# Attention with a parallel MLP: the output tile in two halves, its maxima in pairs, and score-value bursts of four

## The chip, the cores and the metric

The kernel runs on one core of one Trainium2 chip. The metric is the device time of one execution in microseconds, median over runs. The profile is one further execution, taken by the hardware profiler; it has its own time.

A core has TensorE (PE, matrix products into PSUM; PEld is its loading of weights), ScalarE (ACT, exponentials and other functions), VectorE (DVE, element-wise work and 32 x 32 transposes), GpSimd (POOL) and SyncE (SP, here the issuer of nearly all DMAs). Each takes its instructions in the order of the program. PSUM holds what TensorE writes: here eight banks of 128 x 512 fp32 values.

## What is computed

x has 2048 rows of 448. The result is x + A(xn) + B(xn), with xn the layer norm of x.

```
xn = layernorm(x)
A: q = xn @ wq  (16 heads of 28),  k = xn @ wk, v = xn @ wv  (one head of 28, shared by all)
   p = softmax(q @ k.T * 28 ** -0.5);  A = concat(p @ v) @ wo
B: y = layernorm(xn);  B = gelu(y @ w1 + b1) @ w2 + b2       (448 -> 1792 -> 448)
out = x + A + B          (y is a norm of a norm: B normalises xn once more)
```

## The kernel before

The program has three stretches. The first normalises x, and makes queries, keys and values. The second is the MLP; its result, with x and b2 added, goes to memory as `ad`. The third, from about 344 us on, is the attention, and all of the change lies there.

**Units and steps.** A unit is a chunk of 512 query rows and a group of four heads: `NU` = 4 x 4 = 16 units, u = 0 to 15, chunk c = u // 4. A unit has 16 key tiles of 128 (`kt`), and for each key tile and each of the four heads (`j`) one score tile of 128 keys x 512 queries. The main loop (L904) goes over the units and, in each, over eight steps i = 0 to 7. The text calls them the first to the eighth.

**A score** (`score`, L695) is one matmul of 128 x 512 (L703) into a PSUM bank from `mtile`, and an exponential by ScalarE (L704) out of the bank into half of a pair tile `p`, of which there are `PAIRS` = 12. **A score-value product** (`pv`, L889) takes the four heads of one key tile: on TensorE it shows as 8 matmuls with 128 x 32 weights (L894), adding to the one bank `po` for the unit. They come in bursts at the end of a step (letter P): a burst of two key tiles is 16 matmuls. The value products run two key tiles behind the scores, so the burst of the first step ends the unit before.

**Maxima.** The exponent needs an upper estimate of each query's largest score. `max_job` (L529) multiplies the queries with the first 128 keys (matmul L533), transposes the bank to SBUF in 32 x 32 blocks (L540, into a tile `tt`) and takes maxima of the blocks (L541). It is run for unit u + 2 in unit u, one head per step, in the fourth to seventh step. `load_max` in the eighth step joins the maxima and sends their negatives into two rows of the query tile. The same `tt` tiles serve a unit later as scores of key tile 0: `shift_jobs(u + 1)` subtracts the maxima (VectorE, L545), takes the exponential (ScalarE, L548), and transposes back (VectorE, L554). It starts in the third step and goes on by one stage at each X or Y.

**PSUM banks.** `po` has one of the eight. `mtile` hands out the other seven in turn, three from the pool `mp` and four from `ring`, so that a request gets the bank of seven requests before. Scores, maxima and output tiles all come from there. A matmul into a bank waits until ScalarE (a score) or VectorE (a maximum, an output tile) has read what lay there.

**The output tile.** `o_part` (L774) multiplies the finished attention rows of the chunk before with wo: for 128 rows and four groups three matmuls each of 128 x 448 (L781 to L783, high and low parts), twelve in one bank. VectorE adds them to the row of `ad` in a tile `a` (L786), and SyncE sends it out (L787). Each unit from u = 4 on has one such tile, in the sixth step, in place of that step's burst; the seventh step then has a burst of four. The last chunk's four tiles come at the end (`end_jobs`).

**The normalisation** (`norm_jobs`, L818) of a finished unit goes step by step at the letter n: copy of `po` (L821), sum check (L800), transpose, reciprocal, transpose (L826 to L829), product (L832), rounding (L834) and, on GpSimd, the low part (L836).

**The order** inside a step is a string with one letter per action, written by hand; each engine then takes its share in that order. s is a score, M a maximum job, n one stage of the normalisation, X and Y one stage of the shift, e the joining of maxima, o the first output part of the last unit, and P the output tile or the burst:

```
ORDER = "YnsMssnsXsossseP"
SHARES = (8, 8, 8, 7, 7, 7, 7, 8)
```

`SHARES` are the scores of each step, 60 in a unit. SyncE fetches at the start of unit u the row of `ad` that the output tile needs (`load_rows_of`) and then the queries of unit u + 2 in four transfers (`load_q`).

Of the kernel before, what the change touches and what calls it, by code (L numbers as in the profile page):

```python
# [8 lines left out]
F32 = mybir.dt.float32  # L9
F32R = mybir.dt.float32r  # L10
AF = mybir.ActivationFunctionType
ALU = mybir.AluOpType
AX = mybir.AxisListType
PSUM = bass.MemoryType.PSUM

P = 128
S, D, H, DH, F = 2048, 448, 16, 28, 1792
NT = S // P
CT = 4
NCH = NT // CT  # L20
CW = CT * P
NG = H // 4
# [8 lines left out]
MLP_ORDER = (2, 3, 0, 1)  # L31
ENGINES = [mybir.EngineType.PE, mybir.EngineType.Activation, mybir.EngineType.DVE, mybir.EngineType.SP]
ORDER = "YnsMssnsXsossseP"
SHARES = (8, 8, 8, 7, 7, 7, 7, 8)
GELU = 0.044715, 0.7978845608028654
NH = 8
HD = D // 2
# [3 lines left out]
def block_kernel(ctx, tc, x, wq, wk, wv, wo, w1, b1, w2, b2, out):  # L41
    nc = tc.nc
    pe, act, dve, pool = nc.tensor, nc.scalar, nc.vector, nc.gpsimd
# [66 lines left out]
    def mtile(shape):  # L110
        if rings:
            given.append(0)
            if len(given) % 7 > 3 or len(given) % 7 == 0:
                return rings[0].tile(shape, F32, name="m")
        return mp.tile(shape, F32, name="m")
# [300 lines left out]
    for c, at in ((2, ((0, 1), (0, 2), (0, 2), (0, 3))), (3, ((1, 0), (1, 1), (1, 2), (1, 3)))):  # L416
        for k in range(CT):
            later(*at[k], lambda t=CT * c + k: bn(t))
        g = bn_end(c)
# [106 lines left out]
    def blocks_of(t):  # L526
        return t.rearrange("p (b i) -> p b i", i=32)

    def max_job(u, j):  # L529
        if j == 0:  # L530
            mrs[u] = keep.tile([P, 4 * NT], F32, name="mr2", bufs=2)
        pm = mtile([P, CW])
        pe.matmul(pm, km, qss[u][:, j, :], start=True, stop=True)  # L533
        if u == 0:
            if j == 0:
                lasts.append(f(xl_p.tile([P, 4, CW], F32R, name="xl")))
            tts[u, j] = lasts[0][:, j]
        else:
            tts[u, j] = att.tile([P, CW], F32, name="tt", bufs=5)
        dve.transpose(tts[u, j], pm)  # L540
        dve.tensor_reduce(mrs[u][:, NT * j:NT * j + NT], blocks_of(tts[u, j]), axis=AX.X, op=ALU.max)  # L541

    def first_shift(u, j):
        tt = blocks_of(tts[u, j])
# [219 lines left out]
    rows = {}  # L764

    def load_rows_of(c, tiles):
        for k in tiles:
            rows[c, k] = keep.tile([P, D], F32, name="a", bufs=4)
            dve.memset(rows[c, k][0:1, 0:1], 0.0)
            nc.sync.dma_start(rows[c, k], ad[:, CT * c + k, :])  # L770
# [3 lines left out]
    def o_part(c, k, gs):  # L774
# [9 lines left out]
        if gs[-1] == NG - 1:  # L784
            a = rows[c, k]
            dve.tensor_add(a, a, parts.pop((c, k)))  # L786
            (nc.scalar if k % 2 and c == NCH - 1 else nc.sync).dma_start(ov[:, CT * c + k, :], a)  # L787

    def o_jobs(c):
        for k in range(CT):  # L790
            o_part(c, k, range(NG))
            yield
# [107 lines left out]
    xside = Stream()  # L900
    pvq = [(u, kt) for u in range(NU) for kt in range(NT)]
    last = NU * NT // 2 - 1
    o_steps = {(u, 5): (u // NG - 1, u % NG) for u in range(NG, NU)}
    for u in range(NU):  # L904
        todo = [(u, kt, j) for kt in range(1 if u else 2, NT) for j in range(4)]
        for i in range(NT // 2):
            n = NT // 2 * u + i
            if n >= last - 1:
                load_rows_of(NCH - 1, (range(CT - 1), [CT - 1])[n - last + 1])
            for v, step in o_steps:  # L910
                if v == u and i == 0:
                    load_rows_of(o_steps[v, step][0], [o_steps[v, step][1]])
            if n == 9:
                load_wo()
            if 12 <= n < 12 + NG:
                prep_wo(n - 12)
            if i == 0 and u + 2 < NU:
                load_q(u + 2)
            jobs = todo[:SHARES[i] if u else 8 * (i > 0)]
            todo = todo[len(jobs):]  # L920
            maxima = [(u + 2, i - 3 - (u == 0))] if 3 + (u == 0) <= i < 7 + (u == 0) else []
            if u == 0 and i in (1, 2):
                maxima = [(1, 2 * i - 2), (1, 2 * i - 1)]
            for what in ORDER:
                if what == "s" and jobs:
                    score(*jobs.pop(0))
                elif what == "M":
                    for v, j in maxima:
                        if v < NU:
                            max_job(v, j)  # L930
                elif what in "XY":
                    if what == "X" and i == (2 if u else 3) and u + 1 < NU:
                        xside.add(shift_jobs(u + 1))
                    xside.step()
                elif what == "e":
                    if i == 7 and u + 2 < NU:
                        load_max(u + 2)
                    if n == 2:
                        load_max(1)
                elif what == "n":  # L940
                    side.step()
                elif what == "o":
                    if n == last:
                        o_part(NCH - 1, 0, range(NG - 1))
                elif what == "P":
                    assert not jobs
                    if (u, i) in o_steps:
                        o_part(*o_steps[u, i], range(NG))
                        continue
                    for _ in range((BURST if n else 0) * (1 + ((u, i - 1) in o_steps))):  # L950
                        pv(*pvq.pop(0))
        assert not todo
# [85 lines left out]
```

## Time and profile before

| | |
|---|---|
| median of 3 runs | 889.86 us (889.65 to 890.04) |
| profiled execution | 889.81 us, of which the span of the instructions is 888.0 us |
| granted TensorE clock, mean | 0.998 |
| busy share of the span: TensorE, ScalarE, VectorE, GpSimd | 99%, 79%, 55%, 8% |
| the costliest group: exponentials (L704), 956 of them | 489.8 us of ScalarE |
| score matmuls (L703), 960 | 268.8 us of TensorE |
| score-value matmuls (L894), 2016 | 239.9 us of TensorE |

Times inside the profile are microseconds from the start of the span. In a row of the timeline stand start, length, engine, line, operation, the tile written and the tiles read, the shape, how many instructions the row joins, and in brackets how long the engine rested before and what released it. A row of busy time in a window has the window, its length, and then busy time and number of instructions of TensorE, its weight loads, VectorE, ScalarE and GpSimd, followed by the granted clock, the share of DMA time and GB/s. The end of a matmul is modelled, and successive matmuls overlap; so the distance between starts is what counts on TensorE.

### The profile page before, as it was taken

The page shows a single profiled execution, that of the slowest core. Times are in us where ns is not written, and L with a number is a line of the kernel's source. Part 1 is how long each engine was busy: PE and PEld are TensorE (multiplying, and loading weights), DVE is VectorE, ACT ScalarE, POOL GpSimd, SP SyncE. Part 2 cuts the span into 40 slices and gives each one's busy share as a digit, 9 for nine tenths or more (in the row PEclk, how much of TensorE's full clock was granted, in tenths as well). Part 3 has the DMA queues.
Part 4 walks back from the last instruction along what each step waited for, and adds up shares of the span by engine and source line. Part 5 has one row for each costly group of instructions (what it writes and reads, how often), then busy time and mean ns, then how long its engine had stood idle before and what let it go on. Part 6 is the DMA issues. An engine that isn't in the chain of part 4 may idle for free.

```text
span 888.0 us, 13246 instructions
## 1 busy us (share of the span) xinstructions
PE 879.1 (99%) x4914; PEld 566.8 (64%) x4914; DVE 486.0 (55%) x963; ACT 701.7 (79%) x1334; POOL 73.1 (8%) x82
## 2 busy tenths in 40 slices
PE   9999999999999999999999999999999999999997
PEld 8778888888888887444444554554554554554555
DVE  6757766656556876555464464464463463463212
ACT  5677565545454466999999999999999999999992
POOL 5450000000000002040000000000000000000000
PEclk9999999999999999999999999999999999999999
DMA  9975232022003004031102202201202202200011
GB/s 294 326 250 182 94 117 83 1 94 96 1 5 111 1 11 125 2 79 43 43 1 54 64 11 53 64 11 54 63 11 54 64 11 53 63 12 12 21 36 61
DMA packets 36298, 60.69 MB, mean 68 GB/s; under 512 B 7783, under 2 KB 23349, under 8 KB 35205
## 3 DMA queue, kind: packets, MB, share of 16 engines
q1 hardware_dynamic: 34644, 58.95, 21.8%
q10 hardware_dynamic: 1584, 0.84, 0.4%
q8 instruction: 40, 0.66, 0.3%
q14 instruction: 30, 0.24, 0.1%
HBM read 39.89 MB, written 18.88 MB: 66 GB/s over the span
## 4 chain that ended last, share of the span: by engine, by line
PE 91%; ACT 6%; DVE 2%; issue 1%; DMA 0%; POOL 0%; SPq 0%; ACTq 0%; POOLq 0%
PE m L703 25%; PE po L894 24%; PE ph L178 12%; PE m L637 5%; PE m L640 5%; PE m L643 5%; ACT p L704 5%; PE qp L178 2%; PE m L533 2%; PE m L781 2%; PE m L783 1%; PE m L782 1%; PE ph L181 1%; PE ph L183 1%; PE m L406 1%; PE m L178 1%
## 5 line engine op out<-in xcount | busy, mean ns | idle before, releaser
L704 ACT ACTIVATE p<-m 128x512 f32<-128x512 f32 x956 | 489.8, 746 | 28.7 <-PE m L703 28.2
L703 PE MATMUL m<-xh,ks 128*128 128x512 f32 x960 | 268.8, 409 | 0.6 <-DVE tt L540 0.3
L703 PEld LDWEIGHTS m<-xh,ks 128*128 128x128 f32 x960 | 174.5, 188 | 139.7 <-ACT p L704 70.7
L894 PE MATMUL po<-p,vs 128*32 128x512 f32 x2016 | 239.9, 598 | 0.0
L894 PEld LDWEIGHTS po<-p,vs 128*32 128x32 f32 x2016 | 53.8, 109 | 119.7 <-issue 119.4
L610 ACT ACTIVATE hz<-hx,b1s 128x512 f32<-128x512 f32 x56 | 40.6, 726 | 103.0 <-DVE hx L607 103.0
L540 DVE STREAM_TRANSPOSE tt<-m 128x512 f32<-128x512 f32 x60 | 42.9, 715 | 94.9 <-PE m L533 94.9
L637 PE MATMUL m<-w2h,hh 128*128 128x448 f32 x224 | 81.9, 366 | 0.0
L640 PE MATMUL m<-w2l,hh 128*128 128x448 f32 x224 | 81.8, 365 | 0.0
L643 PE MATMUL m<-w2h,hl 128*128 128x448 f32 x224 | 81.7, 365 | 0.0
L821 DVE COPY oc<-po 128x512 f32<-128x512 f32 x15 | 10.4, 692 | 119.8 <-PE po L894 119.8
L607 DVE TENSOR_TENSOR hx<-ph,xn 128x512 f32<-128x512 f32 x53 | 36.5, 689 | 64.8 <-PE ph L183 64.7
L178 PE MATMUL ph<-xh,w1h 128*128 128x512 f32 x159 | 62.8, 395 | 0.0
L178 PE MATMUL ph<-xl,w1h 128*128 128x512 f32 x159 | 62.3, 392 | 0.0
L178 PE MATMUL ph<-xh,w1l 128*128 128x512 f32 x159 | 62.3, 392 | 0.0
L836 POOL TENSOR_TENSOR otl<-oc,oth 128x512 fp32r<-128x512 f32 x15 | 24.1, 1610 | 463.5 <-DVE oth L834 272.3
L548 ACT ACTIVATE tt<-tt 128x512 f32<-128x512 f32 x60 | 53.3, 888 | 0.0
L614 DVE SCALAR_TENSOR_TENSOR hz<-hz,hx 128x512 f32<-128x512 f32 x56 | 38.8, 693 | 20.9 <-ACT hx L611 20.9
L554 DVE STREAM_TRANSPOSE p<-tt 128x512 f32<-128x512 f32 x60 | 42.1, 702 | 9.4 <-ACT tt L548 9.3
L637 PEld LDWEIGHTS m<-w2h,hh 128*128 128x128 f32 x224 | 42.1, 188 | 5.0
L640 PEld LDWEIGHTS m<-w2l,hh 128*128 128x128 f32 x224 | 42.1, 188 | 4.6
L643 PEld LDWEIGHTS m<-w2h,hl 128*128 128x128 f32 x224 | 42.1, 188 | 3.5
(175 smaller groups left out, 1035.3 us busy)
## 6 DMA issues: line engine op xcount, KB each, us to landing
xh<-qd SPq DMA_DIRECT2D x64, 224.0 KB
qd<-qe SPq DMA_DIRECT2D x22, 256.0 KB
a<-in_A_x_dram SPq DMA_DIRECT2D x20, 224.0 KB
ad<-a SPq DMA_DIRECT2D x16, 224.0 KB
a<-ad SPq DMA_DIRECT2D x16, 224.0 KB
raw<-in_B_w_dram SPq DMA_DIRECT2D x7, 448.0 KB
out_dram<-a SPq DMA_DIRECT2D x14, 224.0 KB
xd<-xh SPq DMA_DIRECT2D x2, 1024.0 KB
```

The lines of the kernel that those rows point to most:

```text
L178: pe.matmul(ps, w, v, start=(n == 0), stop=False)
L540: dve.transpose(tts[u, j], pm)
L548: act.activation(tts[u, j], tts[u, j], AF.Exp, scale=SCALE)
L554: dve.transpose(p0s[u][:, j], tts.pop((u, j)))
L610: act.activation(hz, hx, AF.Square, bias=b1s[:, ft:ft + 1], scale=GELU[0] ** 0.5)
L614: dve.scalar_tensor_tensor(hz, hz, 1.0, hx, op0=ALU.add, op1=ALU.mult)
L637: pe.matmul(m2[k], hh[:, ts], w2h, start=(ft == 0), stop=False)
L640: pe.matmul(m2[k], hh[:, ts], w2l, start=False, stop=False)
L643: pe.matmul(m2[k], hl[:, ts], w2h, start=False, stop=(ft == NF - 1))
L703: pe.matmul(s, ks[:, kt * P:(kt + 1) * P], qss[u][:, j, :], start=True, stop=True)
L704: act.activation(p, s, AF.Exp, scale=SCALE)
L894: pe.matmul(po[32 * j:32 * j + 32, :], vs[:, kt, :], ps.pop((u, kt, j)), start=(kt == 0), stop=(kt == NT - 1))
```

## The change

From unit 4 on:

- The output tile is made in two halves of two head groups each (`o_half`): in the third step and in the fifth, each in a bank of its own, with an add of its own by VectorE. The row is sent after the second. The steps behind them, the fourth and the sixth, have bursts of four; so the unit has six bursts where it had seven.
- The four maxima of unit u + 2 are made in two pairs, in the third and fifth step; these steps have six scores each, all others eight.
- The steps follow new order strings. In the third and fifth step the reduction of the maxima (`tensor_reduce`) is put at the very end, after P and X (letter R), behind the transposes out of the banks and the half's add. In the other steps the shift stage that ScalarE works on stands behind four scores, not ahead of the first.
- The shift of unit u + 1 begins in the second step, not the third.
- `tt` has six buffers, not five.

```diff
--- before.py
+++ after.py
@@ -31,7 +31,9 @@
 MLP_ORDER = (2, 3, 0, 1)
 ENGINES = [mybir.EngineType.PE, mybir.EngineType.Activation, mybir.EngineType.DVE, mybir.EngineType.SP]
 ORDER = "YnsMssnsXsossseP"
+LATE_ORDERS = "nsssnsYsosssXeP", "nsMsnsYsmssPXR"
 SHARES = (8, 8, 8, 7, 7, 7, 7, 8)
+LATE_SHARES = (8, 8, 6, 8, 6, 8, 8, 8)
 GELU = 0.044715, 0.7978845608028654
 NH = 8
 HD = D // 2
@@ -526,7 +528,7 @@
     def blocks_of(t):
         return t.rearrange("p (b i) -> p b i", i=32)
 
-    def max_job(u, j):
+    def max_job(u, j, later=None):
         if j == 0:
             mrs[u] = keep.tile([P, 4 * NT], F32, name="mr2", bufs=2)
         pm = mtile([P, CW])
@@ -536,9 +538,16 @@
                 lasts.append(f(xl_p.tile([P, 4, CW], F32R, name="xl")))
             tts[u, j] = lasts[0][:, j]
         else:
-            tts[u, j] = att.tile([P, CW], F32, name="tt", bufs=5)
+            tts[u, j] = att.tile([P, CW], F32, name="tt", bufs=6)
         dve.transpose(tts[u, j], pm)
-        dve.tensor_reduce(mrs[u][:, NT * j:NT * j + NT], blocks_of(tts[u, j]), axis=AX.X, op=ALU.max)
+
+        def maxima(tt=tts[u, j]):
+            dve.tensor_reduce(mrs[u][:, NT * j:NT * j + NT], blocks_of(tt), axis=AX.X, op=ALU.max)
+
+        if later is None:
+            maxima()
+        else:
+            later.append(maxima)
 
     def first_shift(u, j):
         tt = blocks_of(tts[u, j])
@@ -786,6 +795,19 @@
             dve.tensor_add(a, a, parts.pop((c, k)))
             (nc.scalar if k % 2 and c == NCH - 1 else nc.sync).dma_start(ov[:, CT * c + k, :], a)
 
+    def o_half(c, k, gs):
+        po = mtile([P, D])
+        ts = slice(k * P, (k + 1) * P)
+        for g in gs:
+            oth, otl = ots[c, g]
+            pe.matmul(po, oth[:, ts], woh[:, g, :], start=(g == gs[0]), stop=False)
+            pe.matmul(po, oth[:, ts], wol[:, g, :], start=False, stop=False)
+            pe.matmul(po, otl[:, ts], woh[:, g, :], start=False, stop=(g == gs[-1]))
+        a = rows[c, k]
+        dve.tensor_add(a, a, po)
+        if gs[-1] == NG - 1:
+            nc.sync.dma_start(ov[:, CT * c + k, :], a)
+
     def o_jobs(c):
         for k in range(CT):
             o_part(c, k, range(NG))
@@ -900,36 +922,44 @@
     xside = Stream()
     pvq = [(u, kt) for u in range(NU) for kt in range(NT)]
     last = NU * NT // 2 - 1
-    o_steps = {(u, 5): (u // NG - 1, u % NG) for u in range(NG, NU)}
+    o_steps = {(u, 2 * h + 2): (u // NG - 1, u % NG, range(2 * h, 2 * h + 2)) for u in range(NG, NU) for h in range(2)}
     for u in range(NU):
         todo = [(u, kt, j) for kt in range(1 if u else 2, NT) for j in range(4)]
         for i in range(NT // 2):
             n = NT // 2 * u + i
             if n >= last - 1:
                 load_rows_of(NCH - 1, (range(CT - 1), [CT - 1])[n - last + 1])
-            for v, step in o_steps:
-                if v == u and i == 0:
-                    load_rows_of(o_steps[v, step][0], [o_steps[v, step][1]])
+            if i == 0 and u >= NG:
+                load_rows_of(u // NG - 1, [u % NG])
             if n == 9:
                 load_wo()
             if 12 <= n < 12 + NG:
                 prep_wo(n - 12)
             if i == 0 and u + 2 < NU:
                 load_q(u + 2)
-            jobs = todo[:SHARES[i] if u else 8 * (i > 0)]
+            jobs = todo[:(LATE_SHARES if u >= NG else SHARES)[i] if u else 8 * (i > 0)]
             todo = todo[len(jobs):]
             maxima = [(u + 2, i - 3 - (u == 0))] if 3 + (u == 0) <= i < 7 + (u == 0) else []
+            if u >= NG:
+                maxima = [(u + 2, i - 2), (u + 2, i - 1)] if i in (2, 4) else []
             if u == 0 and i in (1, 2):
                 maxima = [(1, 2 * i - 2), (1, 2 * i - 1)]
-            for what in ORDER:
+            reduces = []
+            for what in LATE_ORDERS[i in (2, 4)] if u >= NG else ORDER:
                 if what == "s" and jobs:
                     score(*jobs.pop(0))
-                elif what == "M":
+                elif what == "M" and u < NG:
                     for v, j in maxima:
                         if v < NU:
                             max_job(v, j)
+                elif what in "Mm":
+                    if u + 2 < NU:
+                        max_job(*maxima[what == "m"], reduces)
+                elif what == "R":
+                    for job in reduces:
+                        job()
                 elif what in "XY":
-                    if what == "X" and i == (2 if u else 3) and u + 1 < NU:
+                    if what == "X" and i == (1 if u >= NG else 2 if u else 3) and u + 1 < NU:
                         xside.add(shift_jobs(u + 1))
                     xside.step()
                 elif what == "e":
@@ -945,7 +975,7 @@
                 elif what == "P":
                     assert not jobs
                     if (u, i) in o_steps:
-                        o_part(*o_steps[u, i], range(NG))
+                        o_half(*o_steps[u, i])
                         continue
                     for _ in range((BURST if n else 0) * (1 + ((u, i - 1) in o_steps))):
                         pv(*pvq.pop(0))
```

## The prediction

> **What bounds the kernel now.** I read the page first, then the time of whole units, then the steps of one unit, and then each engine's order of work inside those steps. Of the page, the first lines below are the busy shares and the chain that ended last.
>
> ```profile
> PE 879.1 (99%) x4914; PEld 566.8 (64%) x4914; DVE 486.0 (55%) x963; ACT 701.7 (79%) x1334; POOL 73.1 (8%) x82
> ...
> PE 91%; ACT 6%; DVE 2%; issue 1%; DMA 0%; POOL 0%; SPq 0%; ACTq 0%; POOLq 0%
> ```
>
> TensorE is the chain: 91% of it. The change touches only units 4 to 15, so the next view is busy time in windows. I cut them where a unit's first matmul starts: units 5 to 13 together, unit 14, and the first seven steps of unit 15. The first column after the window is its length.
>
> ```profile
> 503.14:804.73 301.59, 301.59 (x1841) 153.72 (x1837) 153.25 (x324) 283.81 (x577) 14.59 (x9) 1.00 0.16 42
> 804.73:837.82 33.09, 32.65 (x205) 16.32 (x201) 9.89 (x18) 31.60 (x65) 1.58 (x1) 1.00 0.05 14
> 837.82:866.30 28.48, 28.48 (x180) 14.56 (x176) 4.79 (x13) 26.47 (x54) 1.29 (x1) 1.00 0.11 32
> ```
>
> A full unit takes 301.59 / 9 = 33.51 us. Its TensorE (second number) never rests and its ScalarE (fifth) is busy for 283.81 of 301.59. So TensorE's own order sets the pace, with ScalarE 6% behind it. Unit 7 by its eight steps, in the same view:
>
> ```profile
> 570.13:574.05 3.92, 3.92 (x29) 1.84 (x25) 0.00 (x0) 3.92 (x10) 0.00 (x0) 1.00 0.71 168
> 574.05:577.94 3.89, 3.89 (x29) 1.84 (x25) 3.55 (x7) 3.89 (x9) 0.00 (x0) 1.00 0.17 46
> 577.94:581.86 3.92, 3.92 (x28) 1.84 (x25) 1.15 (x3) 3.92 (x10) 1.67 (x1) 1.00 0.00 0
> 581.86:585.95 4.09, 4.09 (x29) 1.84 (x25) 2.59 (x4) 4.09 (x10) 0.00 (x0) 1.00 0.00 0
> 585.95:589.89 3.94, 3.94 (x28) 1.83 (x24) 2.60 (x4) 3.94 (x10) 0.00 (x0) 1.00 0.02 4
> 589.89:594.31 4.42, 4.42 (x24) 3.79 (x21) 2.60 (x4) 4.42 (x11) 0.00 (x0) 1.00 0.00 0
> 594.31:599.79 5.48, 5.48 (x42) 2.25 (x40) 4.55 (x15) 4.06 (x9) 0.00 (x0) 1.00 0.12 43
> 599.79:603.68 3.89, 3.89 (x29) 1.84 (x25) 0.00 (x0) 3.35 (x7) 0.00 (x0) 1.00 0.31 87
> ```
>
> Steps one to six keep ScalarE busy throughout; only under the burst of four in the seventh, and just after it, does it rest. What a step is made of stands in TensorE's timeline (start, length, line):
>
> ```profile
> 572.19 1.92 PE L894 MATMUL po<-p,vs 128*32 128x512 f32 x16
> ...
> 584.09 1.92 PE L894 MATMUL po<-p,vs 128*32 128x512 f32 x16
> ...
> 591.89 0.37 PE L781 MATMUL m<-woh,oth 128*128 128x448 f32 x1
> ...
> 594.11 0.36 PE L783 MATMUL m<-woh,otl 128*128 128x448 f32 x1
> ...
> 594.77 1.52 PE L703 MATMUL m<-xh,ks 128*128 128x512 f32 x6
> 596.22 3.64 PE L894 MATMUL po<-p,vs 128*32 128x512 f32 x32
> ```
>
> Together with the edges of the step windows, six pieces follow. Eight score-like matmuls between two bursts take 572.19 − 570.13 = 2.06. A burst of two takes 574.05 − 572.19 = 1.86. Eight matmuls after a burst and before the output tile take 591.89 − 589.89 = 2.00. The output tile's twelve take 594.31 − 591.89 = 2.42. Eight after it take 596.22 − 594.31 = 1.91, and a burst of four takes 599.79 − 596.22 = 3.57. So a burst of four is 2 × 1.86 − 3.57 = 0.15 cheaper than two bursts, and eight matmuls with a burst on one side only are 0.06 to 0.15 cheaper than between two. A score group that meets the output tile instead of a burst saves about 0.35 in all.
>
> **The change part by part.**
>
> **Order of bursts.** Before, a unit has one step without a burst (the sixth); after, two (third and fifth), and bursts of four in the fourth and sixth. Burst matmuls, scores, maxima and output matmuls keep their number. With the pieces above: steps one and two 3.92 + 3.89; three 2.00 + 2.42 / 2 = 3.21; four 1.91 + 3.57 = 5.48; five 3.21; six 5.48; seven and eight 3.92 + 3.89. The sum is 33.00, against 33.51: **0.51 less per unit**. About 0.35 is the merged burst, and the rest is stalls that vanish: step four is 4.09 where its twin is 3.92, because its first exponential stands behind a first-key exponential (L548) and a bank comes free late:
>
> ```profile
> 583.67 0.19 PEld L703 LDWEIGHTS m<-xh,ks 128*128 128x128 f32 x1 [0.35 <-ACT p L704]
> ```
>
> That stall costs 584.09 − 581.86 − 2.06 = 0.17, and is the price I use for any stall on a bank that is only just late.
>
> **Does ScalarE keep up?** The new steps three and five give it six exponentials and one L548 in 3.21 us, and steps four and six eight and one in 5.48. The seven banks of `mtile` go round in strict order, so a matmul needs the bank used seven before. ScalarE's timeline:
>
> ```profile
> 582.32 0.81 ACT L548 ACTIVATE tt<-tt 128x512 f32<-128x512 f32 x1
> 582.84 3.72 ACT L704 ACTIVATE p<-m 128x512 f32<-128x512 f32 x7
> 586.18 0.89 ACT L548 ACTIVATE tt<-tt 128x512 f32<-128x512 f32 x1
> ...
> 600.33 4.03 ACT L704 ACTIVATE p<-m 128x512 f32<-128x512 f32 x8 [1.95 <-PE m L703]
> ```
>
> One exponential takes (586.18 − 582.84) / 7 = 0.48 of ScalarE, and L548 takes 582.84 − 582.32 = 0.52. The first of a step starts 600.33 − 599.79 = 0.54 behind its matmul. Count from the first matmul of step three: six exponentials and L548 end their turn at 0.54 + 6 × 0.48 + 0.52 = 3.94, and then step four's first exponential starts, which holds its bank for 0.73 to 0.84 ((4.03 − 0.73) / 7 gives 0.47, and 3.72 − 6 × 0.48 gives 0.84). It frees it at 4.67 to 4.78. The matmul that wants it is step four's eighth, at 3.21 + (594.77 + 1.52 − 0.39 − 594.31 = 1.59) = 4.80. This fits by 0.02 to 0.13. Then comes a burst of 3.57, in which ScalarE finishes (3.94 + 8 × 0.48 + 0.52 = 8.30 of 8.69) and rests, so step five starts clean. No exponential is added: sixty and four L548 per unit, as before.
>
> **VectorE's order.** In the third step the maxima transpose (L540) now stands behind two normalisation operations and, since the shift starts one step sooner, behind a shift (L545).
>
> ```profile
> 577.37 0.69 DVE L832 TENSOR_TENSOR oc<-oc,tr 128x512 f32<-128x512 f32 x1
> 578.10 0.43 DVE L834 CAST oth<-oc 128x512 fp32r<-128x512 f32 x1
> 578.44 0.69 DVE L545 TENSOR_TENSOR tt<-tt,mq 128x512 f32<-128x512 f32 x1
> 582.63 0.72 DVE L540 STREAM_TRANSPOSE tt<-m 128x512 f32<-128x512 f32 x1 [3.50 <-PE m L533]
> ...
> 594.51 0.62 DVE L786 TENSOR_TENSOR a<-a,m 128x448 f32<-128x448 f32 x1 [1.22 <-PE m L783]
> ```
>
> The three now end at 578.44 + 0.69 = 579.13, which is 1.19 into step three (577.94). The transpose of 0.72 ends at 1.91. Its bank is the second of nine used in that step, so the ninth, the output half's, needs it at 2.00: it fits by 0.09. The second maxima bank and the half's own add (0.40 behind the last matmul, 0.62 long) come free at about 2.65 and 4.04, and are wanted near 3.9 and 4.6. The reduces (L541) wait for nothing urgent at the end of the step. Queued behind the first add on VectorE are L554, the next shift and then ScalarE's next L548. They end at 4.04 + 0.70 + 0.69 = 5.43, and ScalarE wants the shift at 3.94 + 4 × 0.48 = 5.86. In step five nothing stands ahead of the transpose. **Cost: nothing while these covers hold**; if one goes, 0.17 at that place. The added half-tile add (0.62) falls into VectorE's idle half.
>
> **SyncE and memory.** The output row leaves one step sooner; its row is now wanted in step three, not six. The maxima matmuls (L533) move from step four to three, so the queries of unit u + 2, which SyncE fetches from the unit's start, are wanted 3.92 sooner, at 577.94 + 0.34 = 578.28. In this unit the transfers were over before:
>
> ```profile
> 575.50:576.50 1.00, 1.00 (x7) 0.35 (x9) 0.97 (x4) 1.00 (x3) 0.00 (x0) 1.00 0.01 4
> 576.50:578.20 1.70, 1.70 (x17) 0.52 (x10) 1.60 (x4) 1.70 (x5) 0.00 (x0) 1.00 0.00 0
> ```
>
> The last packet moved before 576.50, so 1.78 us are left for its signal. I cost this at nothing; the other end is under the rivals.
>
> **One tile more.** `tt` has six buffers for five. Before the fourth step's burst 30 scores less the 4 already used are 26 tiles, that is 13 pairs, in 12 buffers. So its last two exponentials wait for the burst's first matmuls, which start at 3.21 + 1.91 = 5.12, long before ScalarE comes to them (5.86 + 0.52 + 2 × 0.48 = 7.34). Nothing.
>
> **The sum.** With places that fit by under 0.1 us, the stalls per unit lie between 0 and 2 × 0.17 = 0.34; I take 0.05, since every cover is positive by its rows. Units 4 to 13: 10 × (0.51 − 0.05) = 4.6. Unit 14 has no maxima: steps three and five have six matmuls (2.00 − 2 × 0.23 + 1.21 = 2.75), but it still has its L548, so ScalarE's 4.7 to the eighth score replaces TensorE's 2.75 + 1.59 = 4.34. Its unstalled 4 × 3.9 + 2 × (2.75 + 5.48) = 32.1 grows by two times 0.36 + 0.1, to 33.0: 0.1 less than 33.09. Unit 15 has neither, and its first seven steps become 3.92 + 3.89 + 2.75 + 5.48 + 2.75 + 5.48 + 3.92 = 28.19: 0.3 less than 28.48. In all 5.0 off the profiled execution's 889.81, which stands 0.05 from the median of 889.86: **884.8 us**. If no cover fails it is 884.3, and with 0.34 in each of ten units 10 × 0.17 + 0.4 = 2.1 off, or 887.7.
>
> **The rivals.**
>
> **ScalarE or VectorE is just late** at both tight places, in every unit: 887.7, as above. For it: the margins are 0.02 to 0.13. Against: the one stall of that kind in the present unit appears only where L548 stands ahead of the first exponential, and the new order puts it behind three or four.
>
> **Slower: VectorE's queue holds the output half.** The bank of the first maxima tile must be empty 2.00 into step three. If the vector work ahead were longer by one operation of 0.69 (a normalisation that starts a little later, or a shift that waits), the bank would come at 2.60, TensorE would stand 0.60 and then load its weights in the open (0.1): 0.7 in each of ten units is 7 over my forecast, or 891.8. It beats the gain from about 0.4 of lateness. Against: every operation ahead has its row, and the chain starts as before, at the end of the first step's burst.
>
> **The queries' signal comes late.** If it trails the last packet by more than 1.78 us, the maxima matmul stands in TensorE's order, and all behind it, for the excess, ten times: 2.5 us would give 884.8 + 7 = 892. No wait on these loads is on record before, so the trail is not measured here. The Trainium skill, page "DMA: Bandwidth & Descriptors", section "Anatomy of one DMA", puts a fixed cost of about 2.0 us on a DMA and most of it between the last byte and its signal; by that the excess would be at most 0.2 and the time about 887, and no run here shows it yet.
>
> **The merge saves nothing**: the 0.35 is read from one kind of step, and two bursts of four in a row of steps might leave ScalarE so far drained that the next steps pay it back: then only the stall of 0.17 goes, 1.7 and some tenths, about 888. Against: the present eighth step starts from just such a drained ScalarE, and takes 3.89.
>
> **How the numbers follow.** Forecast 0.62 (884.3 to 886 by itself); just late 0.16; merge without gain 0.06; VectorE's queue 0.07; queries 0.05; 0.04 for a better time than 883. The range 883.3 to 888.2 leaves out the two slower cases and the better one, and a little of the merge case. About 0.2%, or 1.8 us, is what a measurement here can tell from no change. Faster by more (under 888.1): 0.62 + 0.16 + 0.04, less a little, 0.80; slower (over 891.6): 0.09; the rest, parts of the merge, queue and query cases, 0.11.
>
> **What would show it.** In the changed trace units 5 to 13 should take 33.0 to 33.1 us each; six bursts per unit, two of them 3.57; steps three and five 3.2, four and six 5.5; six output matmuls in 1.21. L548 and L704 should rest about 0.4 to 1 us at each burst of four. Wrong would be: waits of TensorE's weight loads on L540 ahead of L781-type matmuls in step three (VectorE's queue), on L704 at step four's eighth score (just late), or a rest of TensorE ahead of L533 in step three (queries). If units fall to 33.0 and the whole does not, the tail after unit 15 paid it back.

## The result and the profile after

The changed kernel takes 884.30 us (median of 6 runs, 883.36 to 884.70) against 889.76 us for the kernel before in the same sessions: a ratio of 0.9938, with a 95% interval of 0.9928 to 0.9948. That is 5.5 us less. The forecast was 884.8, in a range of 883.3 to 888.2. The profiled execution took 884.14 us, of which the span is 882.3.

The page of the changed kernel, first the busy shares and then the chain that ended last:

```profile
PE 873.2 (99%) x4914; PEld 568.0 (64%) x4914; DVE 491.2 (56%) x975; ACT 702.6 (80%) x1334; POOL 70.0 (8%) x82
...
PE 93%; ACT 3%; DVE 2%; DMA 1%; issue 0%; ACTq 0%
```

TensorE has the same 4914 matmuls and is still the chain. VectorE has 12 instructions more, the second add of each split tile. The same windows as in the prediction, units 5 to 13, unit 14, and the first seven steps of unit 15:

```profile
502.17:799.00 296.83, 296.83 (x1841) 155.34 (x1837) 156.22 (x333) 284.81 (x578) 11.68 (x9) 1.00 0.16 43
799.00:831.95 32.95, 32.95 (x204) 16.43 (x200) 10.21 (x19) 31.64 (x66) 1.29 (x1) 1.00 0.05 15
831.95:860.18 28.23, 28.23 (x180) 14.68 (x176) 5.42 (x14) 25.69 (x54) 1.29 (x1) 1.00 0.13 42
```

A full unit now takes 296.83 / 9 = 32.98 us, 0.53 less; unit 14 is 0.14 shorter and the stretch of unit 15 0.25. Ten units, with unit 4 counted alike, and these two make 5.7. Unit 7 by its eight steps:

```profile
568.14:572.04 3.90, 3.90 (x29) 1.84 (x25) 0.00 (x0) 3.90 (x10) 0.00 (x0) 1.00 0.84 190
572.04:575.96 3.92, 3.92 (x29) 1.84 (x25) 3.61 (x8) 3.92 (x10) 0.00 (x0) 1.00 0.10 25
575.96:579.12 3.16, 3.16 (x19) 2.74 (x15) 2.31 (x4) 3.16 (x8) 1.30 (x1) 1.00 0.00 0
579.12:584.65 5.53, 5.53 (x42) 2.18 (x40) 4.29 (x7) 5.41 (x12) 0.00 (x0) 1.00 0.00 0
584.65:587.81 3.16, 3.16 (x18) 2.73 (x15) 1.43 (x2) 2.63 (x6) 0.00 (x0) 1.00 0.00 0
587.81:593.29 5.48, 5.48 (x41) 2.25 (x39) 4.85 (x12) 5.36 (x11) 0.00 (x0) 1.00 0.13 45
593.29:597.18 3.89, 3.89 (x28) 1.84 (x24) 0.86 (x6) 3.35 (x7) 0.00 (x0) 1.00 0.08 13
597.18:601.10 3.92, 3.92 (x28) 1.84 (x24) 0.00 (x0) 3.92 (x10) 0.00 (x0) 1.00 0.26 77
```

The steps of 4.09, 3.94, 4.42 and 5.48 have become 3.16, 5.53, 3.16 and 5.48. Step four is 0.05 longer than step six, its twin: that is the tight place at ScalarE which the prediction named. From TensorE's weight loads, the ones ahead of the sixth and the eighth score of the fourth step:

```profile
580.16 0.30 PEld L712 LDWEIGHTS m<-xh,ks 128*128 128x128 f32 x2 [0.17 <-ACT p L713]
580.65 0.19 PEld L712 LDWEIGHTS m<-xh,ks 128*128 128x128 f32 x1 [0.19 <-ACT p L713]
```

Both wait for a bank that ScalarE still holds; the loads of the sixth step have no such wait. ScalarE's timeline behind the first burst of four:

```profile
585.18 1.58 ACT L713 ACTIVATE p<-m 128x512 f32<-128x512 f32 x3 [0.65 <-PE m L712]
```

It finishes the fourth step's exponentials under the burst and rests 0.65 us until the first score of the fifth step. So it carries no delay into that step; behind the second burst of four it rests 0.66. VectorE's order in the third step, which begins at 575.96 (the last normalisation transpose, the shift, two normalisation operations, the pair of maxima transposes, and behind the half's matmuls its add), and from TensorE's timeline the start of the output half:

```profile
574.62 0.71 DVE L851 STREAM_TRANSPOSE tr<-rc 128x512 f32<-128x512 f32 x1
575.25 0.65 DVE L554 TENSOR_TENSOR tt<-tt,mq 128x512 f32<-128x512 f32 x1
575.82 0.68 DVE L854 TENSOR_TENSOR oc<-oc,tr 128x512 f32<-128x512 f32 x1
...
576.88 1.49 DVE L542 STREAM_TRANSPOSE tt<-m 128x512 f32<-128x512 f32 x2
579.32 0.62 DVE L807 TENSOR_TENSOR a<-a,m 128x448 f32<-128x448 f32 x1 [0.95 <-PE m L805]
```

```profile
577.90 0.37 PE L803 MATMUL m<-woh,oth 128*128 128x448 f32 x1
```

The first transpose starts at 576.88. With 1.49 for two that overlap a little, about 0.71 for one, it ends 1.63 us into the step, and the output half starts 1.94 into it.

### The profile page after: what moved, and what is told of

Same layout as the page of the kernel before. It is cut to its first block, busy times and chain, and to the rows that moved or that the text cites. A ratio compares the mean times of both kernels' runs of the same rounds, so it can differ in the third digit from the quotient of the medians.

```text
span 882.3 us, 13226 instructions
## 1 busy us (share of the span) xinstructions
PE 873.2 (99%) x4914; PEld 568.0 (64%) x4914; DVE 491.2 (56%) x975; ACT 702.6 (80%) x1334; POOL 70.0 (8%) x82
## 4 chain that ended last, share of the span: by engine, by line
PE 93%; ACT 3%; DVE 2%; DMA 1%; issue 0%; ACTq 0%
PE m L712 26%; PE po L916 25%; PE ph L180 12%; PE m L649 5%; PE m L646 5%; PE m L652 5%; PE qp L180 3%; ACT p L713 2%; PE m L535 2%; PE ph L183 1%; PE ph L185 1%; PE m L805 1%; PE m L803 1%; PE m L804 1%; PE m L180 1%
## 5 line engine op out<-in xcount | busy, mean ns | idle before, releaser
L713 ACT ACTIVATE p<-m 128x512 f32<-128x512 f32 x956 | 485.5, 696 | 22.1 <-PE m L712 21.8
L916 PE MATMUL po<-p,vs 128*32 128x512 f32 x2016 | 237.4, 597 | 0.0
L858 POOL TENSOR_TENSOR otl<-oc,oth 128x512 fp32r<-128x512 f32 x15 | 20.6, 1372 | 462.2 <-DVE oth L856 430.9
L557 ACT ACTIVATE tt<-tt 128x512 f32<-128x512 f32 x60 | 45.1, 752 | 0.0
```

The lines of the kernel that those rows point to most:

```text
L557: act.activation(tts[u, j], tts[u, j], AF.Exp, scale=SCALE)
L713: act.activation(p, s, AF.Exp, scale=SCALE)
L916: pe.matmul(po[32 * j:32 * j + 32, :], vs[:, kt, :], ps.pop((u, kt, j)), start=(kt == 0), stop=(kt == NT - 1))
```

## The experiments

Where a unit is compared, it is a mean over units 5 to 13 of the profiled execution, from a window between their first matmuls. The diffs are excerpts with the lines that matter.

**One part alone: the shift stage later.** The kernel before, with only the letter Y moved:

```diff
+LATE_ORDER = "nsMssnsYsosssXeP"
-            for what in ORDER:
+            for what in LATE_ORDER if u >= NG else ORDER:
```

> The kernel before, with one thing of the change: from unit 4 on the letter Y (the stage with the first-key exponential L548) stands behind the fourth score of a step and not ahead of the first. Bursts, output tile and maxima stay as before. My theory (the stall of the fourth step comes from that exponential standing ahead): the fourth step falls from 4.09 to about 3.92 and the fifth from 3.94 to 3.92, a unit from 33.51 to 33.3, the whole from 889.8 to about 887.5. Rival A (the whole gain of the change is this stall and not the merged bursts): about 884.3. Rival B (the place of Y does nothing): 889.8.

Measured: 886.81 us (886.71 to 887.24), ratio 0.9967 (0.9954 to 0.9979). In its profile, units 5 to 13, unit 14, and then of unit 8 the fourth step and the sixth up to its output tile:

```profile
502.41:802.00 299.59, 299.59 (x1841) 154.70 (x1837) 156.52 (x324) 284.75 (x577) 14.62 (x9) 1.00 0.16 43
802.00:834.63 32.63, 32.63 (x204) 16.34 (x200) 9.80 (x18) 31.60 (x66) 1.58 (x1) 1.00 0.06 18
614.01:617.90 3.89, 3.89 (x28) 1.85 (x24) 2.09 (x4) 3.89 (x9) 0.00 (x0) 1.00 0.00 0
621.82:623.77 1.95, 1.95 (x13) 1.61 (x9) 1.75 (x4) 1.95 (x5) 0.00 (x0) 1.00 0.00 0
```

A unit takes 299.59 / 9 = 33.29. The stall of the fourth step is gone: it takes 3.89. The matmuls ahead of the output tile take 1.95 and not 2.00, so they had lost a little in the same way. In all it is 0.22 per unit, and 0.46 in unit 14, which I had not counted. So a little over half of the change's gain, 3.1 of 5.5 us, can be had from one letter, and Rival A falls: the other 0.31 per unit needs the rest of the change.

**The bursts not merged.** The changed kernel, with a burst of two in every step:

```diff
                     if (u, i) in o_steps:
                         o_half(*o_steps[u, i])
-                        continue
-                    for _ in range((BURST if n else 0) * (1 + ((u, i - 1) in o_steps))):
+                    for _ in range(BURST if n else 0):
```

> The changed kernel, but with a burst of two in every step: the third and fifth step have their half tile and then a burst, and the bursts of four are gone, so 8 bursts per unit and not 6. My theory (a merged burst saves about 0.35 us): 0.7 per unit more, less the 0.05 stall of the fourth step, in twelve units 7.5 us, about 891.8; a unit of 33.6. Rival (the gain is order inside the steps, a merge saves nothing): 884.3, a unit of 33.0.

Measured: 893.01 us (892.57 to 893.65), ratio 1.0037 (1.0024 to 1.0051): slower than before. The window of its units 5 to 13:

```profile
503.10:807.66 304.56, 304.56 (x1841) 151.95 (x1837) 156.23 (x333) 284.80 (x578) 11.67 (x9) 1.00 0.15 42
```

That is 33.84 a unit, 0.86 more than with merged bursts, where I had expected 0.65. One unit of this run in windows: its third and fourth step together, its fifth and sixth, and its seventh; and from the weight loads of that seventh step the one ahead of the eighth score:

```profile
578.57:587.59 9.02, 9.02 (x58) 4.72 (x54) 6.07 (x11) 7.89 (x17) 1.30 (x1) 1.00 0.00 0
587.59:596.65 9.06, 9.06 (x59) 4.81 (x55) 5.71 (x10) 8.00 (x17) 0.00 (x0) 1.00 0.08 27
596.65:600.64 3.99, 3.99 (x28) 1.84 (x24) 1.98 (x11) 3.99 (x10) 0.00 (x0) 1.00 0.02 3
```

```profile
598.35 0.19 PEld L712 LDWEIGHTS m<-xh,ks 128*128 128x128 f32 x1 [0.25 <-ACT p L713]
```

The changed kernel takes 3.16 + 5.53 = 8.69, 3.16 + 5.48 = 8.64 and 3.89 there. So the two merges are worth 0.33 and 0.42, near my 0.35. The other 0.10 is lost in the seventh step, on a bank that ScalarE still holds, and I had not counted it. A part of what a merge is worth lies in the output half. TensorE's timeline from a half's first matmul to the burst behind it:

```profile
614.38 0.37 PE L803 MATMUL m<-woh,oth 128*128 128x448 f32 x1
...
615.68 1.92 PE L916 MATMUL po<-p,vs 128*32 128x512 f32 x16
```

The half takes 1.30 us here, and 579.12 − 577.90 = 1.22 in the changed kernel, where scores follow. The rival falls. Halving the tile without merging the bursts would have lost time, 3.1 us against the kernel before.

**The maxima one by one.** The changed kernel with halves and merged bursts, but one maximum in each of the third to sixth steps, and seven scores:

```diff
-LATE_ORDERS = "nsssnsYsosssXeP", "nsMsnsYsmssPXR"
-LATE_SHARES = (8, 8, 6, 8, 6, 8, 8, 8)
+LATE_ORDERS = "nsMssnsYsosssXeP", "nsMsnsYssssPXR"
+LATE_SHARES = (8, 8, 7, 7, 7, 7, 8, 8)
-                maxima = [(u + 2, i - 2), (u + 2, i - 1)] if i in (2, 4) else []
+                maxima = [(u + 2, i - 2)] if 2 <= i < 6 else []
-                    if u + 2 < NU:
-                        max_job(*maxima[what == "m"], reduces)
+                    if u + 2 < NU and maxima:
+                        max_job(*maxima[0], reduces if i in (2, 4) else None)
```

> The changed kernel with halves and merged bursts as they are, but the four maxima one by one in the third to sixth step, so that these have seven scores each, not six and eight. My theory (the pairs are what lets ScalarE keep up): in the third step ScalarE has seven exponentials and L548 in 3.2 us; the seventh frees its bank at about 4.7, and the fourth step's matmul of that bank stands at 4.35; 0.45 lost in each of two pairs of steps, 0.9 per unit, 893 in all. Rival (the pairs do nothing): 884.3.

Measured: 893.93 us (893.81 to 893.99), ratio 1.0048 (1.0032 to 1.0063). The window of units 5 to 13, and the first of TensorE's weight loads that wait in a fourth step:

```profile
503.23:808.86 305.63, 305.63 (x1840) 154.60 (x1836) 155.90 (x333) 284.81 (x578) 11.67 (x9) 1.00 0.16 42
```

```profile
617.06 0.19 PEld L712 LDWEIGHTS m<-xh,ks 128*128 128x128 f32 x1 [0.30 <-ACT p L713]
```

33.96 a unit, 0.98 more, that is 0.49 for each pair of steps where 0.45 was calculated. The waits are on banks that ScalarE still holds, in the fourth step, as calculated. So the pairs matter: they keep ScalarE's load in the short steps at six.

**The maxima at once.** The changed kernel with each reduction right behind its transpose, ahead of the second transpose and the add:

```diff
-                        max_job(*maxima[what == "m"], reduces)
+                        max_job(*maxima[what == "m"])
```

> The changed kernel, but each reduction of maxima stands right behind its transpose again, ahead of the second transpose and of the half tile's add. My theory (the banks have room): the second transpose ends near 2.9 us into the third step and the add near 4.2 where its bank is wanted at 4.5, so nothing is late, 884.3 as with the change (within 0.7). Rival (putting the maxima later is part of the gain): 0.2 to 0.35 us per unit are lost in the fourth and sixth step, 886 to 888.

Measured: 883.94 us (883.52 to 884.44), ratio 0.9932 (0.9919 to 0.9946). The interval holds the changed kernel's 0.9938. Taking the maxima later earns nothing that can be measured; the banks had room.

**The shift stage first.** The changed kernel, with Y ahead of the first score in the steps without maxima:

```diff
-LATE_ORDERS = "nsssnsYsosssXeP", "nsMsnsYsmssPXR"
+LATE_ORDERS = "YnsssnssosssXeP", "nsMsnsYsmssPXR"
```

> The changed kernel, but with the stage Y (first-key exponential) ahead of the first score in the steps without maxima, as it was before the change; the steps with maxima keep their order. My theory: in the fourth and sixth step that exponential waits for VectorE's shift, which now comes behind the half tile's add; ScalarE rests about 1.3 us ahead of it, the first exponential's bank is 1.7 us late for the eighth score, and TensorE loses 1.6 to 1.8 us in each of these steps: 3.4 per unit, 35 in all, 915 to 922. Rival (the place of Y costs no more than the old 0.17 us): 886 to 888.

Measured: 920.63 us (two runs, 920.58 and 920.68), ratio 1.0343 (1.0322 to 1.0364). ScalarE's timeline in a fourth step, and the operation of VectorE that it waits for:

```profile
627.88 0.63 ACT L557 ACTIVATE tt<-tt 128x512 f32<-128x512 f32 x1 [1.07 <-DVE tt L554]
628.42 4.00 ACT L713 ACTIVATE p<-m 128x512 f32<-128x512 f32 x8
```

```profile
627.20 0.65 DVE L554 TENSOR_TENSOR tt<-tt,mq 128x512 f32<-128x512 f32 x1
```

```profile
505.64:833.30 327.66, 301.66 (x1840) 155.36 (x1836) 154.55 (x333) 286.71 (x578) 11.68 (x9) 1.00 0.15 39
```

The last row is the window of units 5 to 13: 36.41 a unit, and TensorE, the first busy time, now rests for 26 us of it. ScalarE stands 1.07 us for a shift that comes behind the half's add, and eight exponentials stand behind it. The new place of Y is therefore not only worth 0.2 a unit; with the halves in place it carries 3.4.

**VectorE's queue, one operation more.** Ahead of the first maxima transpose of the third step:

```diff
+    def spend():
+        spent = att.tile([P, D], F32, name="spent", bufs=1)
+        dve.tensor_mul(spent, wor[:, 0, :], wor[:, 0, :])
                     if u + 2 < NU:
+                        for _ in range(1 * (i == 2 and what == "M")):
+                            spend()
                         max_job(*maxima[what == "m"], reduces)
```

> The changed kernel, with one more VectorE operation (a product of 128 x 448, about 0.6 us) ahead of the first maxima transpose of the third step, from unit 4 to 13. It tests the rival of the prediction in which VectorE's queue holds the output half. In the changed profile that transpose ends 1.63 us into the step and its bank is wanted at 1.95. My theory: 0.3 too late, 0.3 to 0.4 per unit with the weight load in the open, 3 to 4 in all, 887.5 to 888.5. Rival (the bank is not what the half tile waits for): 884.3.

Measured: 887.81 us (887.16 to 888.22), ratio 0.9975 (0.9964 to 0.9986). The window of units 5 to 13 and the weight load of the output half in a third step:

```profile
502.76:802.82 300.06, 298.66 (x1840) 155.29 (x1836) 159.11 (x342) 284.93 (x578) 13.97 (x9) 1.00 0.16 42
```

```profile
612.72 0.19 PEld L803 LDWEIGHTS m<-woh,oth 128*128 128x128 f32 x1 [0.54 <-DVE tt L542]
```

33.34 a unit, 0.36 more, with a wait of the named kind. The bank is what the half waits for.

**Two operations more.** The same with `range(2 * ...)`:

> As the run with one VectorE operation ahead of the first maxima transpose, but with two (about 1.2 us). My theory: 0.9 too late, 0.9 to 1.05 per unit in ten units, 893.5 to 895: slower than before the change. Rival: 884.3 if the bank is not waited for; 888 if what follows gives part of it back.

Measured: 904.80 us (903.82 to 906.17), ratio 1.0162 (1.0145 to 1.0179), ten more than expected. VectorE's timeline joins the two products, 2.24 us together where one takes 0.62; GpSimd's has its low part at that time:

```profile
619.69 2.24 DVE L924 TENSOR_TENSOR spent<-wor 128x448 f32<-128x448 f32 x2
```

```profile
619.86 1.60 POOL L858 TENSOR_TENSOR otl<-oc,oth 128x512 fp32r<-128x512 f32 x1 [33.34 <-DVE oth L856]
```

The first product starts ahead of GpSimd's operation and takes 0.62; the second starts beside it and takes 1.59. So the run did not test what it was made for, and I repeated it with operations of one SBUF input.

**Two transposes more.** The two products replaced:

```diff
-        dve.tensor_mul(spent, wor[:, 0, :], wor[:, 0, :])
+        dve.transpose(spent, wor[:, 0, :])
```

> As the run with two VectorE products ahead of the first maxima transpose, but the two are 32 x 32 transposes of 128 x 448 (one SBUF input each). There the second product took 1.59 us in the profile, beside GpSimd's low part, where the first took 0.62. My theory: that length came from GpSimd's work beside it and products with two SBUF inputs; a transpose keeps its 0.62, so the bank is 0.9 to 1.0 late, and ten units lose 1.0 each: 893.5 to 895. Rival (the second operation is slow for another reason, or a late bank costs twice its lateness): about 904 again.

Measured: 894.13 us (893.60 to 894.87), ratio 1.0049 (1.0033 to 1.0064): as calculated, and slower than before the change. The window of units 5 to 13, and VectorE's and GpSimd's timelines at the added operations:

```profile
503.58:809.36 305.78, 298.72 (x1841) 155.31 (x1837) 164.88 (x351) 285.77 (x578) 11.68 (x9) 1.00 0.16 42
```

```profile
614.24 1.32 DVE L924 STREAM_TRANSPOSE spent<-wor 128x448 f32<-128x448 f32 x2
```

```profile
614.40 1.30 POOL L858 TENSOR_TENSOR otl<-oc,oth 128x512 fp32r<-128x512 f32 x1 [32.69 <-DVE oth L856]
```

33.98 a unit, 1.00 more. The transposes take 1.32 together with GpSimd's operation beside them, so it was the second product that was held up, and not any second operation. The prediction's slower rival is a real mechanism with the price it gave; the changed kernel only lies on the right side of it.

**The queries later.** The four transfers for unit u + 2 made to wait for a VectorE memset in the second step:

```diff
-            if i == 0 and u + 2 < NU:
+            if i == (1 if u >= NG else 0) and u + 2 < NU:
+                if u >= NG:
+                    dve.memset(f(qst[(u + 2) % 3])[0:1, 0, 0:1], 0.0)
                 load_q(u + 2)
```

> The changed kernel, but the four transfers with the queries of unit u + 2 wait for a small VectorE memset in the second step, some 5 us later than now, so that the maxima matmul of the third step does have to wait for them. It measures how long the signal trails the last packet. My estimate from the changed kernel, where nothing waits: the trail is under 1.8 us. If it is about 0.5 us, the matmul starts 0.5 us behind the last packet of a unit's transfers; if it is 2 us, the prediction's cover for the queries was nearly used up. TensorE should stand 3 to 6 us in each third step, 920 to 945 in all.

Measured: 915.10 us (one run). TensorE's timeline at the maxima matmul, and windows before, at and behind it; the last two numbers are the share of DMA time and GB/s, and before them the granted clock:

```profile
622.40 0.47 PE L535 MATMUL m<-xh,km 128*128 128x512 f32 x1 [1.85 <-DMA xh<-qd]
```

```profile
620.00:621.50 1.50, 0.55 (x5) 0.19 (x1) 1.03 (x3) 1.24 (x3) 0.35 (x1) 1.00 0.67 198
621.50:622.30 0.80, 0.00 (x0) 0.00 (x0) 0.00 (x0) 0.00 (x0) 0.80 (x1) 1.00 0.00 0
622.30:626.70 4.40, 4.30 (x13) 3.61 (x14) 1.44 (x2) 3.06 (x6) 0.11 (x1) 0.62 0.01 4
```

The DMA share is 0.67 up to 621.50 and 0.00 behind it, and the matmul starts at 622.40: the signal trails by about 0.9 us here, where the prediction had 1.78 to spare. In the ten units, in windows of 0.1 us, it trails by 0.7 to 1.1. The Trainium skill, page "DMA: Bandwidth & Descriptors", section "Anatomy of one DMA", puts most of 2.0 us there. That section is about transfers issued by GpSimd, and these are SyncE's; the measurement decides, and the trail is under half of that. My forecast of the time was missed. I expected 3 to 6 us of standing in each such step and 920 to 945 in all; it was 1.61 to 2.37, together 19.2 us in the ten units. Most of the other 11.6 of the 30.8 us lost is a slower clock behind the rest, in six of the ten (below).

**The early units too.** The changed kernel, with Y behind the fourth score in units 1 to 3 as well:

```diff
+MID_ORDER = "nsMssnsYsosssXeP"
-            for what in LATE_ORDERS[i in (2, 4)] if u >= NG else ORDER:
+            for what in LATE_ORDERS[i in (2, 4)] if u >= NG else MID_ORDER if u else ORDER:
```

> The changed kernel, and units 1 to 3 also have Y behind the fourth score. My theory: the 0.15 to 0.2 us stall of their fourth and fifth steps goes, three times, 0.5 to 0.7 us in all, 883.7; in the profile units 1 to 3 fall from 33.4 or 33.5 to about 33.2 or 33.3 each. Rival (in these units something else makes the stall): 884.3 and no change in those units.

Measured: 884.02 us (883.44 to 884.20), ratio 0.9934 (0.9920 to 0.9947), not to be told from the changed kernel. Units 1 and 4 in its profile, and unit 1 in that of the changed kernel:

```profile
374.47:405.72 31.25, 31.25 (x196) 14.75 (x192) 18.72 (x36) 31.25 (x65) 9.34 (x9) 1.00 0.25 57
468.53:501.93 33.40, 33.32 (x208) 17.25 (x204) 17.45 (x37) 32.07 (x67) 1.29 (x1) 1.00 0.21 55
```

```profile
374.60:406.26 31.66, 31.60 (x197) 14.72 (x193) 17.63 (x36) 31.66 (x66) 9.44 (x9) 1.00 0.25 57
```

My expectation had these units at 33.4 or 33.5 us, but unit 1 takes 31.66 in the changed kernel. It gains 0.41, but ScalarE is busy for every microsecond of it (31.25 of 31.25, and 31.66 of 31.66 in the changed kernel). As I read it, TensorE only runs further ahead of ScalarE, and unit 4 gives the time back: 33.40 where the changed kernel has 33.02. I had sought the stall in the order; in unit 1 the bound is ScalarE's own work.

**Unit 14 the old way**, with its output tile whole in the sixth step and seven scores in steps four to seven, on top of the last run; the order, the maxima and the start of the shift go by `paired[u]` as the shares do:

```diff
+    paired = [NG <= u != NU - 2 for u in range(NU)]
+    o_steps = {(u, 2 * h + 2): (u // NG - 1, u % NG, range(2 * h, 2 * h + 2))
+               for u in range(NG, NU) for h in range(2) if paired[u]}
+    o_steps[NU - 2, 5] = (NCH - 2, 2, range(NG))
...
-            jobs = todo[:(LATE_SHARES if u >= NG else SHARES)[i] if u else 8 * (i > 0)]
+            jobs = todo[:(LATE_SHARES if paired[u] else SHARES)[i] if u else 8 * (i > 0)]
...
```

> The changed kernel with units 1 to 3 also having the shift stage behind the fourth score, and unit 14 (which has no maxima) with its output tile whole in the sixth step and seven scores in steps four to seven, in that same order. My theory: unit 14 falls from 32.95 to about 32.6 as in the run with only that stage moved, and unit 1 from 31.66 to 31.25, with 0.1 from units 2 and 3: 0.9 in all, 883.4. Rival (what unit 14 gains the next unit gives back): 884.0.

Measured: 883.49 us (883.29 to 884.16), ratio 0.9932 (0.9918 to 0.9946). Unit 14:

```profile
798.87:831.45 32.58, 32.58 (x205) 16.33 (x201) 9.80 (x18) 31.55 (x66) 1.58 (x1) 1.00 0.05 15
```

Unit 14 falls from 32.95 to 32.58 as forecast, and the first seven steps of unit 15 do not give it back: 859.70 − 831.45 = 28.25, against 28.23. The median is the lowest of all runs, but the intervals of this run and the last both hold the changed kernel's ratio: better by its profile, by four tenths in one unit, and not to be told from the changed kernel by the times.

## Why the prediction was right, point by point

**Order of bursts.** The eight pieces summed to 33.00 a unit, 33.05 with the 0.05 for stalls; 32.98 was measured. The misses are small and partly cancel. The matmuls ahead of a half take 1.94 (577.90 − 575.96), and not 2.00, in both steps. The run with one letter moved shows why: the old 2.00 held a little of the stall that goes with Y, and that stall was worth 0.22 in all and not 0.16. The merge's 0.35 lies between the 0.33 and 0.42 of the run without merged bursts. By causes that gives 0.22 + 0.35 − 0.05 = 0.52, where 0.53 was measured.

**ScalarE keeps up.** The calculation gave 0.02 to 0.13 of room at the fourth step's eighth score, and the fourth step lost 0.05. The calculation compared the moment at which the bank comes free with the start of the matmul, but the weight load ahead of the matmul waits for the bank as well: by 0.17 at the sixth score and 0.19 at the eighth, most of it hidden behind other matmuls. The run with one maximum per step shows that the account holds where it is overdrawn: 0.98 lost per unit, for 0.9 calculated.

**VectorE's order.** The bank was to come free 1.91 into the third step and did so at 1.63; the room was 0.31 and not 0.09. The prediction put the shift behind the two normalisation operations; it runs ahead of them. That changes two terms. The old trace showed the shift beside GpSimd's low part, at 0.69; ahead of that it takes 0.65, and the next operation follows its start by 0.57 (575.82 behind 575.25). And the shift starts 0.63 behind the last normalisation transpose (574.62), where in the kernel before the product stood there and started 0.74 behind it (577.37 behind 576.63). These are 0.12 and 0.11 of the 0.28. One operation more costs 0.36, two cost 1.0; the mechanism was right, and the changed kernel is further from it than I said.

**Cost of stalls.** 0.05 per unit is what the profile shows at the fourth step. The prediction chose that value between 0 and 0.34 without a row for it, so that it fits so well is luck.

**Units 14 and 15.** Forecast 0.1 and 0.3, measured 0.14 and 0.25. The account of unit 14 was that ScalarE, which has its L548 as before but no maxima to lighten the short steps, comes late for the scores behind each half, by 0.36 and 0.1 more. The eight scores behind the first half in unit 14 and in unit 15, which has no L548, and a weight load in the former:

```profile
809.52:811.93 2.41, 2.41 (x10) 1.24 (x8) 1.81 (x3) 2.41 (x6) 0.00 (x0) 1.00 0.00 0
842.47:844.48 2.01, 2.01 (x10) 1.24 (x8) 0.62 (x1) 2.01 (x5) 0.00 (x0) 1.00 0.00 0
```

```profile
811.01 0.30 PEld L712 LDWEIGHTS m<-xh,ks 128*128 128x128 f32 x2 [0.30 <-ACT p L713]
```

It is 0.40 longer, waiting for ScalarE. With the old tile unit 14 takes 32.58.

**Queries, tile buffer, output row.** No matmul or weight load waits for them in the attention of the changed profile; the queries' signal, measured by itself, trails by about 0.9 us of the 1.78.

**The sum** was 5.0 and is 5.5 in the medians; 5.7 in these units of the two profiled executions. What lies outside them differs by some tenths between executions of the same code: from the eighth step of unit 15 to the end it is 22.1 us in the changed kernel (882.3 − 860.18) and 22.4 in the last run above (882.1 − 859.70). I do not assign it.

**The rivals.** "Just late" holds at a third of its price and only at one place. The merge without gain fell. VectorE's queue is real but not reached: the bank has 0.31 to spare. The queries are not reached either.

## What to carry to other kernels

Where one engine never rests, sum its order piece by piece from the old trace, with the pieces that stand next to the same neighbours; then ask of each buffer, in the new order, who frees it and by when. A switch between two kinds of matmul that costs 0.3 to 0.4 us is worth merging away only if the engine that reads the banks can live with the longer stretches: here the paired maxima made that possible, and without them the kernel was 4 us slower than before the change. A time that shrinks in a unit where another engine is busy throughout may only be moved, as in unit 1 here.

## What the runs showed of the hardware

**A VectorE product beside a GpSimd operation.** A product with two SBUF inputs took 0.62 us where it started ahead of GpSimd's low part, and 1.59 where it started beside it (2.24 for the two); transposes with one input did not lengthen (1.32 for two). GpSimd's low part lengthens too where it starts beside such a product: 1.30 beside transposes, 1.60 beside the products, and in the kernel before, beside the shift:

```profile
578.61 1.67 POOL L836 TENSOR_TENSOR otl<-oc,oth 128x512 fp32r<-128x512 f32 x1 [31.83 <-DVE oth L834]
```

So by moving the shift ahead, the change also took it out of GpSimd's way (the low part takes 1.30 in the changed kernel's third step), which neither its description nor my account had.

**The clock after a short rest.** In the run with the late queries TensorE rested 1.85 us in the third step of the unit shown, and the granted clock was 0.62 in the 4.4 us behind it, as its last window shows. It did not happen each time. In the unit before, TensorE's timeline and the window behind the rest are these:

```profile
587.39 0.47 PE L535 MATMUL m<-xh,km 128*128 128x512 f32 x1 [2.11 <-DMA xh<-qd]
```

```profile
587.30:591.70 4.40, 4.31 (x20) 3.68 (x20) 2.65 (x5) 3.58 (x8) 0.00 (x0) 1.00 0.00 0
```

Here a longer rest was followed by the full clock. Of the ten rests of that run, six were followed by a clock of 0.62 to 0.71 for some 4 us (rests of 1.61 to 2.37) and four by 1.00 (1.87 to 2.11). In the run with two products it was one rest of ten (1.83), and nine of 1.73 or 1.74 were followed by 1.00. So a rest of about 2 us can cost over 1 us more than itself: from the third step's first matmul to the end of its output half it was 6.8 us in the slow unit and 5.5 in the other. What decides between the two these runs leave open; the length of the rest alone does not.
